# Identity, one weight load, the norm's small steps and the planner's limits in a planned attention and MLP kernel

## The chip, the cores and the metric

The kernel runs on one core of a Trainium2 chip. The metric is device time in microseconds (us). The kernel before takes 758.47 us, the median of 3 runs (757.53 to 758.52).

## The reference

`x` is 2048 rows of 512 numbers in bf16 (batch 1). Two branches work on it and a gate mixes them:

```
def _A_ref(x, wqkv, wo):          # 32 heads of 16
    q, k, v = split(x @ wqkv)
    p = softmax(q k^T * 16**-0.5)
    return concat(p v) @ wo
def _B_ref(x, w1, w2, w3, w4):    # F = 1792
    h  = gelu(layernorm(x) @ w1)
    x1 = x + shifted(h) @ w2      # four column quarters shifted by 1, -1, 2, -2 rows
    return x1 + gelu(layernorm(x1) @ w3) @ w4
g = sigmoid((x * gate_w).sum(-1)) # one number per row
out = g * _A_ref(x) + (1 - g) * _B_ref(x)
```

Gelu is the tanh approximation; the layer norms have no weights.

## The kernel before

**Tiling.** Everything is bf16 with f32 sums. The 2048 rows form 16 tiles of 128 (`x_sb`) and 4 chunks of 512. `xT` is x transposed: chunk 0 is made on TensorE by 16 transposes against a 128x128 identity (L1505), chunks 1 to 3 by DMA transposes (L150). A head unit is one chunk of queries by four heads; there are 4 x 8 = 32 units, each with 64 blocks of scores (16 key tiles by 4 heads, 128x512 each).

**The main loop.** TensorE (PE) computes two or three score blocks into a PSUM tile `stage` (L865); ScalarE (ACT) exponentiates the tile in one instruction into a ring of bf16 tiles (L1264); PE multiplies by the values and sums in `acc` (L1277). Not all blocks go to ACT. Whole groups of four heads go another way: their scores land in `dsc`, VectorE (DVE) turns them into 16-bit integers (L1082), three further terms come from adding a constant, on DVE (L1147) or on GpSimd (POOL, an INT64_ADD, L1145), and all four integer tiles (`quad`, `lent`, `more`, `xT` are the buffers) are read as bf16 by the value products, with plain (`vp`) or weighted values (`vw`).

**The rest of the work** is put between these slots: the projections, and the MLP branch. Its norms need per row mean and variance (`bn_stats`, `bn_aggr` at L440), the reciprocal root by an integer guess and three rounds of three steps (L460 to L466), the normalized tiles `xn` (L472) and their transposes `xnT`, four DMA transposes per chunk on SP's queue (L485). `ps_y` is a product of `xnT` with the first MLP weights (`w12`) or with `w3`.

**What sets the order.** A planner inside the kernel, run while the program is built, keeps a clock per engine (`free`), estimated costs and due times (`at`), and always takes the next step that could begin first; ties go by rank. It only writes the order down: on the chip each engine runs its instructions in that order, and waits on semaphores. DVE's small steps stand in one list `asides`, taken one at a time when their key says they are ready. `dma(t, own, count)` is its model of SP's queue, where each DMA has a fixed cost of issue. `rule(name)` reads limits per unit: from `RULES` for units 1 to 31, from `USUAL` for unit 0 and for names that `RULES` leaves out. `NEED` is how many blocks of a unit must be left for a group of it to go to DVE, `DLIM` how much work DVE may have queued, `CHAINS` how many groups may be open, `HURRY` and `AHEAD` when their steps gain rank, `MANY`, `PTS` and `SHORT` when value products come ahead of other work, `KEEP`, `BACK`, `PMAX` how add steps are shared between DVE and POOL. Where PE would idle too long, `fill` puts in matmuls with a zero tile.

**The start** is written out by hand. DMAs for the first tiles go out on SP and ACT (L123 to L125). DVE builds the identity from a ramp: it doubles a row of numbers seven times (L135), takes a 32x32 transposed column (L137) and compares in four strips (L140). POOL sets constant tiles meanwhile (L141 to L155), requests a set of programs (`load_library`, L163), which the INT64_ADD needs, and goes on. On SP the load of `wkv`'s value half (L148) waits for POOL's memset of wkv's last column (L146), and the input transposes (L150) for its memset of one element of xT (L147). PE runs 8 matmuls on a zero tile first (L1501), then the transposes against the identity.

**Weights.** `w12` is loaded at the start of the MLP (L562, L563), right ahead of the first four `xnT` transposes. `w3` (1792 KB) follows when its room is free (L764), `w4` (1792 KB) at L590.

Of the kernel before, what the change touches and what calls it, by code (L numbers as in the profile page):

```python
# [9 lines left out]

# [9 lines left out]
EPS = 1e-5  # L20
# [12 lines left out]
def kernel(  # L33
# [96 lines left out]
    ramp = const.tile([P, P], F32, name="ramp")  # L130
    row = const.tile([P, 32], F32, name="row")
    nc.vector.memset(ramp[:, 0:1], 0.0)
    w = 1
    while w < P:
        nc.vector.tensor_scalar(out=ramp[:, w:2 * w], in0=ramp[:, 0:w], scalar1=float(w), scalar2=None, op0=ALU.add)  # L135
        if w == 16:
            nc.vector.transpose(out=row[:], in_=ramp[:, 0:32])  # L137
        w *= 2
    for o in range(0, P, 32):
        nc.vector.tensor_scalar(out=ident[o:o + 32, :], in0=ramp[o:o + 32, :], scalar1=float(-o), scalar2=row[o:o + 32, 0:1], op0=ALU.add, op1=ALU.is_equal)  # L140
    nc.gpsimd.memset(zero[:], 0.0)  # L141
    nc.gpsimd.memset(vp0[:], 0.0)
# [20 lines left out]
    nc.gpsimd.load_library(library_config.all_libraries[1])  # L163
# [7 lines left out]
    for j in range(4):  # L171
# [10 lines left out]
        1: {'NEED': 12, 'AHEAD': 8, 'HURRY': 24, 'DLIM': 0.6, 'PTS': 6, 'CHAINS': 6, 'MAXD': 24, 'PMAX': 2, 'BACK': 0.6, 'KEEP': 0.6},  # L182
        2: {'NEED': 12, 'AHEAD': 8, 'HURRY': 24, 'DLIM': 0.6, 'PTS': 6, 'CHAINS': 6, 'MAXD': 24, 'PMAX': 2, 'BACK': 0.6, 'KEEP': 0.6},
        3: {'NEED': 12, 'AHEAD': 8, 'HURRY': 24, 'DLIM': 0.6, 'PTS': 6, 'CHAINS': 6, 'MAXD': 24, 'PMAX': 2, 'BACK': 0.6, 'KEEP': 0.6},
        4: {'NEED': 12, 'AHEAD': 8, 'HURRY': 24, 'DLIM': 0.6, 'PTS': 6, 'CHAINS': 6, 'MAXD': 24, 'PMAX': 2, 'BACK': 0.6, 'KEEP': 0.6},
        5: {'NEED': 12, 'AHEAD': 8, 'HURRY': 24, 'DLIM': 0.6, 'PTS': 6, 'CHAINS': 6, 'MAXD': 24, 'PMAX': 2, 'BACK': 0.6, 'KEEP': 0.6},
        6: {'NEED': 12, 'AHEAD': 8, 'HURRY': 24, 'DLIM': 0.6, 'PTS': 6, 'CHAINS': 6, 'MAXD': 24, 'PMAX': 2, 'BACK': 0.6, 'KEEP': 0.6},
        7: {'NEED': 12, 'AHEAD': 8, 'HURRY': 24, 'DLIM': 0.6, 'PTS': 6, 'CHAINS': 6, 'MAXD': 24, 'PMAX': 2, 'BACK': 0.6, 'KEEP': 0.6},
        8: {'NEED': 12, 'AHEAD': 8, 'HURRY': 24, 'DLIM': 0.6, 'PTS': 6, 'CHAINS': 6, 'MAXD': 24, 'PMAX': 2, 'BACK': 0.6, 'KEEP': 0.6},
        9: {'NEED': 12, 'AHEAD': 8, 'HURRY': 24, 'DLIM': 0.6, 'PTS': 6, 'CHAINS': 6, 'MAXD': 24, 'PMAX': 2, 'BACK': 0.6, 'KEEP': 0.6},  # L190
        10: {'NEED': 12, 'AHEAD': 8, 'HURRY': 24, 'DLIM': 0.6, 'PTS': 6, 'CHAINS': 6, 'MAXD': 24, 'PMAX': 2, 'BACK': 0.6, 'KEEP': 0.6},
        11: {'NEED': 12, 'AHEAD': 8, 'HURRY': 24, 'DLIM': 0.6, 'PTS': 6, 'CHAINS': 6, 'MAXD': 24, 'PMAX': 2, 'BACK': 0.6, 'KEEP': 0.6},
        12: {'NEED': 12, 'AHEAD': 8, 'HURRY': 24, 'DLIM': 0.6, 'PTS': 6, 'CHAINS': 6, 'MAXD': 24, 'PMAX': 2, 'BACK': 0.6, 'KEEP': 0.6},
        13: {'NEED': 12, 'AHEAD': 8, 'HURRY': 24, 'DLIM': 0.6, 'PTS': 6, 'CHAINS': 6, 'MAXD': 24, 'PMAX': 2, 'BACK': 0.6, 'KEEP': 0.6},
        14: {'NEED': 12, 'AHEAD': 8, 'HURRY': 24, 'DLIM': 0.6, 'PTS': 6, 'CHAINS': 6, 'MAXD': 24, 'PMAX': 2, 'BACK': 0.6, 'KEEP': 0.6},
        15: {'NEED': 12, 'AHEAD': 8, 'HURRY': 24, 'DLIM': 0.6, 'PTS': 6, 'CHAINS': 6, 'MAXD': 24, 'PMAX': 2, 'BACK': 0.6, 'KEEP': 0.6},
        16: {'NEED': 12, 'AHEAD': 8, 'HURRY': 24, 'DLIM': 0.6, 'PTS': 6, 'CHAINS': 6, 'MAXD': 24, 'PMAX': 2, 'BACK': 0.6, 'KEEP': 0.6},
        17: {'NEED': 12, 'AHEAD': 8, 'HURRY': 24, 'DLIM': 0.6, 'PTS': 6, 'CHAINS': 6, 'MAXD': 24, 'PMAX': 2, 'BACK': 0.6, 'KEEP': 0.6},
        18: {'NEED': 12, 'AHEAD': 8, 'HURRY': 24, 'DLIM': 0.6, 'PTS': 6, 'CHAINS': 6, 'MAXD': 24, 'PMAX': 2, 'BACK': 0.6, 'KEEP': 0.6},
        19: {'NEED': 12, 'AHEAD': 8, 'HURRY': 24, 'DLIM': 0.6, 'PTS': 6, 'CHAINS': 6, 'MAXD': 24, 'PMAX': 2, 'BACK': 0.6, 'KEEP': 0.6},  # L200
        20: {'NEED': 12, 'AHEAD': 8, 'HURRY': 24, 'DLIM': 0.6, 'PTS': 6, 'CHAINS': 6, 'MAXD': 24, 'PMAX': 2, 'BACK': 0.6, 'KEEP': 0.6},
        21: {'NEED': 12, 'AHEAD': 8, 'HURRY': 24, 'DLIM': 0.6, 'PTS': 6, 'CHAINS': 6, 'MAXD': 24, 'PMAX': 2, 'BACK': 0.6, 'KEEP': 0.6},
# [222 lines left out]
    ROOT = 0.18  # L425
    root_x, root_z = ([const.tile([P, NT if n == 0 else 4], F32, name=f"root_{k}{n}") for n in range(2)] for k in "xz")
    xns = {}

    def aside(cost, fn, key=None, shared=False):
        asides.append((cost, fn, key, shared))  # L430

    def ln_stats(n, t):
        st = {}

        def stats(end):
            st[0] = stat.tile([P, 6], F32, tag="bnst", name="st")
            nc.vector.bn_stats(out=st[0][:], in_=x_sb[t][:])
# [1261 lines left out]
```

## Time and profile before

| | |
|---|---|
| median of 3 runs | 758.47 us |
| profiled execution, its own time | 762.97 us |
| span of the profile | 761.2 us |
| mean granted TensorE clock | 0.986 |
| busy: PE, ACT, DVE, POOL | 736.3, 721.9, 674.0, 313.4 us |
| ACT's first score exponential begins | 13.72 us |
| PE waits for `xnT` | 4.5 us, 2 times |
| PE waits for the identity | 2.5 us, once |

In the profile a row of the waits gives engine, output and line, then what it waited for, the total in us, the times and the longest. A row in order of time gives start, duration, engine (SPq is the queue that issues SP's DMAs), line, operation, and in brackets the idle time before it. In the table by stretches the numbers behind each stretch are the busy us of PE, weight loads, DVE, ACT and POOL (with instruction counts), the granted clock of TensorE, the DMA share and GB/s. The ends of matmuls are modelled.

### The profile page before, as it was taken

Reading aid. Unit: us, or ns where it says so; the run is one execution under the profiler, and the core shown is the slowest. Engines: PE = TensorE matmul, PEld = TensorE weight load, DVE = VectorE, ACT = ScalarE, POOL = GpSimd, SP = SyncE. Lnnn points to the kernel's source line nnn. Section 1 sums busy time; section 2 is a strip of 40 time slices with the busy share of each in tenths; the row PEclk is TensorE's granted clock in tenths of the full one; section 3 lists DMA queues with packets and bytes.
Section 4 is the critical chain, followed back from the end, with each engine's and each line's share of the span. In section 5 each row is a group of like instructions: output and inputs, shape, how many; then the busy total and the mean of one; then the engine's idle time right before and its main releaser. Section 6 shows DMA issues by size and latency. Waiting matters only on the chain.

```text
span 761.2 us, 23457 instructions
## 1 busy us (share of the span) xinstructions
PE 736.3 (97%) x9805; PEld 225.3 (30%) x9806; DVE 674.0 (89%) x1231; ACT 721.9 (95%) x729; POOL 313.4 (41%) x329
## 2 busy tenths in 40 slices
PE   7999998999999998999999999999999999999997
PEld 3433322222332222232222232222322222232223
DVE  6989997999989996999999888899798989979974
ACT  4999998999999996899999999999999999999995
POOL 2024344445434323435544435453454544545540
PEclk9999998999999997999999999999999999999999
DMA  8300007101130025002001010000020000000001
GB/s 221 92 4 24 16 20 102 41 23 45 37 111 22 19 74 77 19 17 34 20 20 48 19 37 16 22 16 20 20 51 26 30 11 20 19 31 20 20 24 39
DMA packets 52306, 29.02 MB, mean 38 GB/s; under 512 B 36712, under 2 KB 47720, under 8 KB 52200
## 3 DMA queue, kind: packets, MB, share of 16 engines
q1 hardware_dynamic: 51240, 27.00, 14.8%
q8 instruction: 76, 1.25, 0.7%
q10 hardware_dynamic: 960, 0.52, 0.2%
q14 instruction: 30, 0.25, 0.1%
HBM read 17.17 MB, written 2.35 MB: 26 GB/s over the span
## 4 chain that ended last, share of the span: by engine, by line
PE 59%; DVE 18%; ACT 15%; issue 4%; SPq 2%; DMA 2%; DVEq 0%; ACTq 0%
PE acc L1277 20%; PE stage L865 18%; ACT ring L1264 11%; PE ps L323 8%; DVE quad L1082 4%; PE ps_y L323 4%; ACT pt L1264 3%; DVE more L1082 3%; PE stage L323 2%; SPq L485 2%; PE ps_o L323 2%; DVE xT L1082 1%; DMA xnT<-xn 1%; PE ps_q L323 1%; DVE oT L1386 1%
## 5 line engine op out<-in xcount | busy, mean ns | idle before, releaser
L1264 ACT ACTIVATE ring<-stage 128x1024 bf16<-128x1024 f32 (+1 forms) x648 | 641.1, 1116 | 18.0 <-PE dsc L865 11.8
L865 PE MATMUL stage<-qT,kT 16*128 16x512 bf16 (+2 forms) x1506 | 271.3, 384 | 5.7 <-ACT ring L1264 2.6
L865 PE MATMUL dsc<-qT,kT 16*128 16x512 bf16 (+1 forms) x566 | 219.3, 388 | 2.8 <-DVE quad L1082 1.7
L1082 DVE TENSOR_SCALAR quad<-dsc 128x512 int16<-128x512 f32 x242 | 161.3, 686 | 15.3 <-PE dsc L865 13.0
L865 PEld LDWEIGHTS <-kT 16*128 16x128 bf16 (+1 forms) x2072 | 73.5, 91 | 285.9 <-issue 260.7
L1277 PE MATMUL acc<-ring,vp 128*17 128x512 bf16 (+3 forms) x1408 | 125.6, 381 | 0.5 <-DVE accsb L1359 0.2
L1082 DVE TENSOR_SCALAR more<-dsc 128x512 int16<-128x512 f32 x147 | 98.0, 685 | 15.8 <-PE dsc L865 14.0
L1082 DVE TENSOR_SCALAR xT<-dsc 128x512 int16<-128x512 f32 x133 | 88.3, 684 | 8.4 <-PE dsc L865 7.7
L1145 POOL INT64_ADD quad<-quad x58 | 62.1, 1072 | 51.1 <-PE acc L1277 14.8
L1277 PEld LDWEIGHTS <-vp 128*17 128x17 bf16 (+1 forms) x2668 | 55.4, 89 | 78.4 <-issue 57.0
L323 PE MATMUL ps<-w,g2T 128*32 128x512 bf16 x896 | 67.4, 384 | 0.3 <-DVE ot L645 0.3
L323 PE MATMUL ps_y<-xnT,w 128*32 128x512 bf16 x704 | 56.3, 402 | 5.1 <-DMA xnT<-xn 4.5
L1145 POOL INT64_ADD xT<-quad x33 | 34.6, 1051 | 52.3 <-DVE more L1147 17.4
L1145 POOL INT64_ADD quad<-more x31 | 32.1, 1038 | 57.0 <-DVE quad L1147 25.4
L1277 PE MATMUL acc<-quad,vp 128*17 128x512 bf16 x516 | 48.4, 382 | 0.3 <-DVE quad L1147 0.3
L1277 PE MATMUL acc<-quad,vw 128*17 128x512 bf16 x492 | 47.2, 385 | 0.0
L1145 POOL INT64_ADD quad<-xT x28 | 29.0, 1038 | 38.2 <-DVE more L1147 16.4
L1145 POOL INT64_ADD more<-more x35 | 36.3, 1038 | 17.3 <-PE dsc L865 6.5
L1145 POOL INT64_ADD more<-quad x23 | 23.9, 1038 | 45.2 <-DVE quad L1147 27.2
L1277 PEld LDWEIGHTS <-vw 128*17 128x17 bf16 x1192 | 27.0, 89 | 38.2 <-issue 31.5
L323 PEld LDWEIGHTS <-w 128*32 128x32 bf16 x1152 | 25.3, 96 | 43.3 <-issue 26.0
L1264 ACT ACTIVATE pt<-stage 128x1024 bf16<-128x1024 f32 x34 | 31.4, 1094 | 1.2 <-PE stage L865 1.1
(148 smaller groups left out, 900.6 us busy)
## 6 DMA issues: line engine op xcount, KB each, us to landing
bcs<-rec_d SPq DMA_DIRECT2D x31, 256.0 KB
w<-in_B_w_dram SPq DMA_DIRECT2D x2, 1792.0 KB
x_sb<-in_A_x_dram SPq DMA_DIRECT2D x14, 128.0 KB
oT<-oT SPq DMA_DIRECT2D x112, 16.0 KB
out_dram<-ot SPq DMA_DIRECT2D x12, 128.0 KB
w<-in_B_w_dram SPq DMA_DIRECT2D x2, 512.0 KB
wkv<-in_A_wqkv_dram SPq DMA_DIRECT2D x1, 512.0 KB
wo_all<-in_A_wo_dram SPq DMA_DIRECT2D x8, 64.0 KB
```

The lines of the kernel that those rows point to most:

```text
L323: nc.tensor.matmul(out[j:j + 32, :], lhsT=lhsT[:, j:j + 32], rhs=rhs, tile_position=(0, j), **kwargs)
L485: nc.sync.dma_start(out=xnT[:, :, j * P:(j + 1) * P], in_=xns.pop((n, 4 * c + j))[:], transpose=True)
L865: nc.tensor.matmul(out, lhsT=kT[G][32 * j:32 * j + K, cc, o:o + P], rhs=qTs[(c, G)][32 * j:32 * j + K, a, lo:hi], start=True, stop=True, t ...
L1082: nc.vector.tensor_scalar(out=bits[:, r:r + wide, :], in0=dsc.rearrange("p (a c) -> p a c", c=CH), scalar1=SHIFT, scalar2=LOWEST, op0=ALU. ...
L1145: behind(nc.gpsimd.int64_add(out=words(to), in0=words(base["tile"]), in1=int(shift) * 0x0001000100010001))
L1264: nc.scalar.activation(out=pt[:, 0:w], in_=stages.pop(k)[:, 0:w], func=ACT.Exp, scale=LN2 / 128.0)
L1277: nc.tensor.matmul(accs[n][32 * j:32 * j + M, lo:hi], lhsT=lhsT, rhs=p, start=(kt == 0), stop=(kt == NT - 1), skip_group_check=True, tile_ ...
L1386: nc.vector.tensor_tensor(out=oT, in0=tiles["accsb"][:], in1=tiles["bcs"][:], op=ALU.mult)
```

## The change

Five edits. The identity is made on POOL by the library's helper (a memset and an AFFINE_SELECT, a masked copy by row and column), with the request for the set of programs ahead of it; DVE's ramp goes. The load of `w4` is written behind the transposes of the second norm's first chunk. Each `bn_aggr` and each root step gets a key `apart`, which lets the planner start it only 0.02 us after its estimate of the end of the step before. In the planner's model of SP's queue the transposes that follow the `w12` load cost 2.0 us each and not 1.3, until `at["heavy"]`. And the limits of units 1 to 31 are new (the 31 rows are alike, before and now).

```diff
-    ramp = const.tile([P, P], F32, name="ramp")
-    row = const.tile([P, 32], F32, name="row")
-    nc.vector.memset(ramp[:, 0:1], 0.0)
-    w = 1
-    while w < P:
-        nc.vector.tensor_scalar(out=ramp[:, w:2 * w], in0=ramp[:, 0:w], scalar1=float(w), scalar2=None, op0=ALU.add)
-        if w == 16:
-            nc.vector.transpose(out=row[:], in_=ramp[:, 0:32])
-        w *= 2
-    for o in range(0, P, 32):
-        nc.vector.tensor_scalar(out=ident[o:o + 32, :], in0=ramp[o:o + 32, :], scalar1=float(-o), scalar2=row[o:o + 32, 0:1], op0=ALU.add, op1=ALU.is_equal)
+    nc.gpsimd.load_library(library_config.all_libraries[1])
     nc.gpsimd.memset(zero[:], 0.0)
+    make_identity(nc, ident[:])
     nc.gpsimd.memset(vp0[:], 0.0)
...
-    nc.gpsimd.load_library(library_config.all_libraries[1])
...
-        1: {'NEED': 12, 'AHEAD': 8, 'HURRY': 24, 'DLIM': 0.6, 'PTS': 6, 'CHAINS': 6, 'MAXD': 24, 'PMAX': 2, 'BACK': 0.6, 'KEEP': 0.6},
+        1: {'NEED': 20, 'HURRY': 16, 'DLIM': 0.9, 'MANY': 10, 'PTS': 6, 'CHAINS': 3, 'MAXD': 24, 'PMAX': 2, 'BACK': 0.6, 'SHORT': -1, 'KEEP': 0.9},
...
+    def apart():
+        return state["aside"] + 0.02
+
...
-        aside(0.18, lambda end: nc.vector.bn_aggr(out=mvs[n][:, t, :], in_=st[0][:]))
+        aside(0.18, lambda end: nc.vector.bn_aggr(out=mvs[n][:, t, :], in_=st[0][:]), apart)
...
             for fn in (square, share_of, last if k == 2 else better):
-                aside(ROOT, fn)
+                aside(ROOT, fn, apart)
...
-        at["xnT", n, c, KT - 1] = at["xnfree"] = dma(state["t"], 1.3, 4) + XPOSE - 5.2 + MARGIN
+        at["xnT", n, c, KT - 1] = at["xnfree"] = dma(state["t"], 1.3 if state["t"] > at["heavy"] else 2.0, 4) + XPOSE - 5.2 + MARGIN
...
-        at["w12"] = state["t"] + 9.0
+        at["w12"] = at["heavy"] = state["t"] + 9.0
...
-        w4 = hw.tile([P, FT, D], BF16, tag="hw", name="w4")
-        nc.sync.dma_start(out=w4[:], in_=wview(B_w4))
-        at["w4"] = state["t"] + 16.0
         if w3 is None:
             yield lambda: 0.0 if retired["n"] == 3 else None
             w3 = load_w3()
         res = []
         yield from norm_T(1, 0, res)
+        w4 = hw.tile([P, FT, D], BF16, tag="hw", name="w4")
+        nc.sync.dma_start(out=w4[:], in_=wview(B_w4))
+        at["w4"] = state["t"] + 16.0
```

The order of the instructions at the places of which the prediction speaks (lines are those of each kernel's own file). POOL at the start, before: the end of the constant tiles, the copy of the identity, the request (the second row of kind ISA here is already the first INT64_ADD):

```order
L152 MEMSET pick 128x4
L154 MEMSET pick 1x1 x4
L155 CAST identf<-ident 128x128
L163 ISA
L421 MEMSET mhalf 128x1
L1535 COPY wkv<-gw 128x4
L1145 ISA lent<-quad_286 128x1024
```

and POOL at the start now:

```order
L131 ISA
L132 MEMSET zero 128x128
masks.py:197 MEMSET ident 128x128
masks.py:199 AFFINE_SELECT ident<-ident 128x128
L134 MEMSET vp_142 128x1024
L135 MEMSET vp_142 128x32
```

The request stood behind everything on POOL and is now first; the identity is POOL's third step, and the value tiles' memsets follow it.

SP's queue at the second norm, before: denominators (`den`), their reciprocals out and back (`rec_d`, `bcs`), w4 (`w_5794`), the transposes, four pieces of a head's output (`oT`):

```order
L1367 DMA den<-accsb 128x1x16
L1375 DMA rec_d<-rec 128x16
L1376 DMA bcs<-rec_d 128x1x512
L590 DMA w_5794<-in_B_w_dram 128x14x512
L485 DMA_TRANSPOSE xnT<-xn 128x4x128 x4
L1395 DMA oT_282<-oT 16x512 x4
```

and now:

```order
L1361 DMA den<-accsb 128x1x16
L1369 DMA rec_d<-rec 128x16
L1370 DMA bcs<-rec_d 128x1x512
L479 DMA_TRANSPOSE xnT<-xn 128x4x128 x4
L589 DMA w_5790<-in_B_w_dram 128x14x512
L1389 DMA oT_271<-oT 16x512 x4
```

The 1792 KB load has changed places with the four transposes; its neighbours are the same.

More of the change, by code (lines that the diff above doesn't have):

```diff
@@ L9 @@
 from concourse._compat import with_exitstack
+from concourse.masks import make_identity
 ACT = mybir.ActivationFunctionType
@@ L186 @@
[L186 to L197, printed above, removed]
@@ L213 @@
+        30: {'NEED': 20, 'HURRY': 16, 'DLIM': 0.9, 'MANY': 10, 'PTS': 6, 'CHAINS': 3, 'MAXD': 24, 'PMAX': 2, 'BACK': 0.6, 'SHORT': -1, 'KEEP': 0.9},
+        31: {'NEED': 20, 'HURRY': 16, 'DLIM': 0.9, 'MANY': 10, 'PTS': 6, 'CHAINS': 3, 'MAXD': 24, 'PMAX': 2, 'BACK': 0.6, 'SHORT': -1, 'KEEP': 0.9},
     }
```

52 lines of the change are left out of this document (31 added, 21 removed).

## The prediction

> **What bounds the kernel now.** I read the busy shares first, then the table of 10-us stretches, then the waits of each engine, and last the instructions in order of time around the long waits and at the start. The busy shares:
>
> ```profile
> span 761.2 us, 23457 instructions
> PE 736.3 (97%) x9805; PEld 225.3 (30%) x9806; DVE 674.0 (89%) x1231; ACT 721.9 (95%) x729; POOL 313.4 (41%) x329
> ```
>
> PE and ACT are both nearly full, and of the two ACT is the one whose share can be trusted, since the ends of matmuls are modelled. ACT's work is fixed in size (exponentials of the scores that DVE and POOL do not take), so time is lost where ACT stands idle, 761.2 - 721.9 = 39.3 us in all. Stretches with the busy time of PE, PEld, DVE, ACT, POOL, then the granted clock, DMA share and GB/s show where:
>
> ```profile
> 123.00:129.60 6.60, 4.68 (x59) 1.43 (x51) 5.65 (x10) 5.77 (x7) 4.25 (x4) 0.97 1.41 110
> 129.60:136.80 7.20, 7.16 (x60) 1.44 (x60) 3.91 (x6) 4.44 (x4) 2.37 (x3) 0.55 0.02 5
> 150.00:255.00 105.00, 102.19 (x1335) 31.20 (x1327) 99.41 (x177) 104.82 (x108) 48.92 (x47) 1.00 0.17 46
> 282.00:291.40 9.40, 9.18 (x104) 2.50 (x103) 9.40 (x21) 9.20 (x10) 3.74 (x4) 1.00 1.44 230
> 291.40:296.00 4.60, 1.90 (x15) 0.37 (x15) 1.86 (x5) 1.23 (x2) 2.46 (x3) 0.68 0.21 45
> 296.00:301.00 5.00, 5.00 (x41) 1.01 (x37) 3.30 (x6) 3.45 (x4) 0.00 (x0) 0.50 0.01 1
> 301.00:306.00 5.00, 5.00 (x45) 1.14 (x41) 2.60 (x7) 2.65 (x3) 1.49 (x2) 0.50 0.04 6
> 306.00:312.00 6.00, 5.96 (x77) 1.48 (x70) 5.57 (x14) 5.65 (x6) 2.44 (x3) 0.94 0.12 44
> 343.70:437.50 93.80, 93.24 (x1249) 26.09 (x1249) 86.20 (x142) 93.30 (x96) 45.14 (x43) 1.00 0.11 28
> ```
>
> In 150 to 255 ACT is idle 0.18 us of 105, in 343.7 to 437.5 0.50 of 93.8: there it is the bound. Between 123.0 and 136.8 it is idle 13.80 - 5.77 - 4.44 = **3.59 us**, and between 282 and 312 30.00 - 9.20 - 1.23 - 3.45 - 2.65 - 5.65 = **7.82 us**. In both PE stops first and then runs at a granted clock of 0.50 to 0.68, so that ACT starves although PE reads as full. PE's waits and its instructions name the cause:
>
> ```profile
> PE ps_y L323 <- DMA xnT<-xn: 4.5, 2, 2.7
> PE ps_t L1505 <- DVE ident L140: 2.5, 1, 2.5
> 129.65 0.62 PE L323 MATMUL ps_y<-xnT,w 128*32 128x512 bf16 x4 [1.77 <-DMA xnT<-xn]
> 294.10 0.62 PE L323 MATMUL ps_y<-xnT,w 128*32 128x512 bf16 x4 [2.71 <-DMA xnT<-xn]
> ```
>
> Both times the first matmuls on a chunk's transposed norm wait for the DMA transposes, 1.77 and 2.71 us. SP's queue shows why they are late:
>
> ```profile
> 116.81 0.39 SPq L562 DMA_DIRECT2D w<-in_B_w_dram  x1
> 117.79 7.96 SPq L485 DMA_TRANSPOSE xnT<-xn  x4
> 178.00 5.15 SPq L485 DMA_TRANSPOSE xnT<-xn  x4
> 186.18 0.39 PE L323 MATMUL ps_y<-xnT,w 128*32 128x512 bf16 x4
> 279.40 0.42 SPq L590 DMA_DIRECT2D w<-in_B_w_dram  x1
> 279.87 10.29 SPq L485 DMA_TRANSPOSE xnT<-xn  x4
> ```
>
> With nothing ahead, four transposes issue in 5.15 us and are read by PE 8.18 us after the first began (186.18 - 178.00), without a wait. Behind the first-layer weights they take 7.96 us to issue, behind w4 10.29 us, and PE reads them 11.86 and 14.23 us after the first.
>
> **The change, part by part.** *w4 behind the transposes.* In SP's order the w4 load now stands behind the four transposes of the second norm's first chunk, which have only small transfers just ahead of them. Their landing goes from 14.23 us back to at most 8.18. The order keeps ten score slots on PE between issue and first use, before and now; a slot costs ACT 93.8 / 96 = 0.98 us in the stretch from 343.7, so they cover 9.8 us. The wait and its slow clock should go: **-7.8 us**. What is late instead is w4, by about 5 us; it is first read by the second layer's last product, after the Gelu that starts at 333.18, some 50 us later:
>
> ```profile
> 333.18 1.28 ACT L1241 ACT_TABLE_LOAD   x1
> ```
>
> With that cover gone it would cost those 5 us.
>
> *Transposes costed at 2.0 us behind the first weights.* The queue keeps the loads ahead of the transposes. The planner now expects them later: PE's order has 14 score slots between their issue and first use where it had 10, and they are the program's own work brought forward. Four slots are 3.9 us, the wait was 1.77, so it is covered with about 2 us over: **-3.6 us**. If the landing slips by as much again, nothing is gained here; a loss would need a landing 3.9 us later.
>
> [...]
>
> *Identity on GpSimd.* The start, in order of time:
>
> ```profile
> 0.73 0.20 POOL L141 MEMSET zero<- 128x128 bf16 x1 [0.29 <-POOLq L1683]
> 1.19 4.31 DVE L135 TENSOR_SCALAR ramp<-ramp 128x1 f32<-128x1 f32 x5
> 1.19 3.60 PE L1501 MATMUL warm<-ring 128*128 128x512 bf16 x8 [1.19 <-DVE ramp L132]
> 2.16 1.28 ACT L1507 ACT_TABLE_LOAD   x1 [2.16 <-issue]
> 3.77 0.40 POOL L146 MEMSET wkv<- 128x1 bf16 x1
> 4.21 0.37 SPq L148 DMA_DIRECT2D wkv<-in_A_wqkv_dram  x1
> 7.28 1.87 PE L1505 MATMUL ps_t<-ident,x_sb 128*128 128x128 bf16 x16 [2.50 <-DVE ident L140]
> 7.37 0.29 POOL L155 CAST identf<-ident 128x128 f32<-128x128 bf16 x1 [1.77 <-DVE ident L140]
> 7.76 0.10 POOL L421 MEMSET mhalf<- 128x1 f32 x1
> 14.40 0.40 PE L323 MATMUL ps_v<-wkv,xT 128*32 128x256 bf16 x8 [0.71 <-DVE qT L1543]
> 20.18 0.51 SPq L169 DMA_DIRECT2D gw<-in_gate_w_dram  x1
> 25.39 0.20 POOL L1535 COPY wkv<-gw 128x4 bf16<-128x4 bf16 x1 [17.52 <-DMA wo_pad<-in_A_wo_dram]
> 49.41 1.04 POOL L1145 INT64_ADD lent<-quad  x1 [23.82 <-DVE quad L1147]
> ```
>
> Removed are thirteen short DVE instructions from the ramp to the four comparisons, which end at 7.2; PE stood idle 2.50 us for them after its warm-up (1.19 + 3.60 = 4.79). Added on POOL are a memset (0.20 us, as zero) and a selection over the same 128x128 (0.29 us, as identf), now behind the request for the set of programs. How long that request holds the selection the trace does not show: a plain memset ran right behind it at 7.76, and the first instruction that needs the set came only at 49.41, so it took under 41.7 us. From below, PE cannot start before 4.79, so the gain is at most **2.5 us**; that is the case if it costs what ACT's table load costs (1.28). From above, 41.7 us would make the start some 36 us later. The nearest row I see is a fetch into the crowded start: gw's, 25.39 - 20.18 = 5.21 us from issue to use. By it the identity stands at 0.73 + 5.21 + 0.20 + 0.29 = 6.4 and PE starts 0.8 us earlier: **-0.8 us**. [...]
>
> Behind the selection on POOL's queue stand the memsets of the value tiles, of wkv's last column and of xT, and behind these, on SP's queue, the load of wkv's value half (4.21 before), the three input transposes and all later loads. They slip by about 5.5 us (6.4 - 0.9). The cover is the time until their first reader: wkv was issued at 4.21 and read at 14.40, 10.2 us later, so 3.9 us would remain (13.6 - 9.7) where a fetch like gw's needs 5.21. Up to 1.3 us could show; but wkv's half now comes first on a queue that has been idle since the first tiles, so I take **0**, with 0 to +5.5 (no cover at all) as bounds.
>
> *Steps set apart, new limits.* Counting instructions of both orders: 149 groups of four heads that DVE and POOL exponentiate become 148, so ACT gets two more 1024-wide exponentials; at the pitch of the first 34 (31.51 / 34 = 0.93) that is **+1.9 us**.
>
> ```profile
> 13.72 31.51 ACT L1264 ACTIVATE pt<-stage 128x1024 bf16<-128x1024 f32 x34 [1.07 <-PE stage L865]
> L1145 POOL INT64_ADD quad<-quad x58 | 62.1, 1072 | 51.1 <-PE acc L1277 14.8
> 45.00:752.40 707.40, 691.14 (x9218) 205.74 (x9211) 634.58 (x1113) 687.81 (x691) 307.95 (x296) 0.99 0.14 32
> ```
>
> DVE does 148 of the add steps instead of 153, POOL 296 instead of 294 (1.07 us each), neither of them the bound. Setting a bn_aggr or root step behind the end of the one before lets other DVE work between them: nothing on the path. Between 45 and 752.4 ACT is idle 707.40 - 687.81 = 19.6 us, 11.4 of it in the two places. The 8.2 us left are scattered waits, and the new order may halve them or add half again: **0**, bounds -4 to +4. PE's order has 216 filler matmuls where it had 184, which hide in waits.
>
> Sum: -7.8 - 3.6 - 0.8 + 1.9 = **-10.3 us**. The profiled execution took 762.97 us (span 761.2), so it would take 752.7. It is 4.5 us above the median of the runs, 758.47. If the runs have the same stalls, they come to 758.47 - 10.3 = 748.2; if all of the 4.5 sits in the two stalls, to 752.7. I lay a third of it there: **749.7 us**.
>
> **Rivals.** *One stall stays.* The loads still stand ahead of the first transposes, and the slots that cover them are a plan. Then 758.47 - 10.3 + 3.6 = 751.8 with the first, or 756.0 with the second left. For it: both stalls came from plans that thought they covered them. Against it: 2.1 and 1.6 us to spare.
>
> *New stalls from the new limits.* Every due time shifts; a PE gap of 1.8 us cost 3.6 us, one of 2.7 us 7.8. Two new gaps take 7 us back: about 756.5. Against it: in the two long stretches of the table, 199 us together, no PE wait took the clock below 1.00.
>
> *The request holds POOL too long.* Mechanism: the selection waits, PE has no identity, the memsets behind it hold SP's loads. Each us past 6.0 (where PE starts as before) is a us of ACT idle. Slower than before begins where the request takes about 5.2 + 10.3 = 15.5 us; at 20 us the time is 764. For it: nothing in the trace bounds it below 41.7. Against it: every fetch at the start lands within 6 us.
>
> *The change does not do what it says:* w4 could be held by hT's readers anyway and the transposes pass unhindered before too. The 10.29 us issue against 5.15 excludes that.
>
> **How the numbers follow.** Forecast (both stalls gone, start about as before) 0.65; one stall stays 0.14; new stalls 0.12; the request too long, slower 0.07; no effect 0.02. The range from 743 to 757 holds the forecast's bounds (749.7 - 1.7 for the start, - 4 for the limits, - 1; and the same limits upward) and most of the two rivals that take part of the gain back. A measurement of this kernel tells a change of 0.2%, 1.5 us, from none. Slower than 760.0 is the third rival and little else: 0.07. Within 0.2%: the far ends of rivals one and two, and no effect, 0.06. Faster: 0.87.
>
> **What would show it.** Right: PE's wait for xnT gone from its list or under 0.3 us; granted clock 1.00 in the stretches of both norms; the four transposes of the second norm issued in about 5.2 us; ACT idle about 27 us in all. PE's first transposes between 4.8 and 7.3, and the value half of wkv issued near 9.7. Wrong: a clock near 0.5 after any later gap, a PE start past 9 us, or waits for wkv or xT on PE between 14 and 30.

## The result, and the profile after

The changed kernel takes **750.98 us**, the median of four runs (748.32 to 751.88), against 758.26 us (757.53 to 758.52, four runs) for the kernel before: a ratio of **0.990, 95% interval 0.9874 to 0.9926**. The forecast was 749.7. Its profiled execution took 748.32 us, the shortest of its four, where the one of before (762.97) was longer than all its others; so the two profiles stand 14.65 us apart, and the medians 7.3.

First the busy shares after, then the table by stretches (start and end, length, busy us of PE, weight loads, DVE, ACT and POOL with instruction counts, granted clock, DMA share, GB/s) around the two norms:

```profile
span 746.5 us, 23512 instructions
PE 727.2 (97%) x9826; PEld 226.5 (30%) x9826; DVE 659.7 (88%) x1209; ACT 723.0 (97%) x731; POOL 316.4 (42%) x333
...
112.00:125.00 13.00, 12.93 (x164) 3.86 (x166) 12.68 (x22) 13.00 (x15) 7.49 (x10) 1.00 0.96 144
125.00:137.00 12.00, 11.88 (x162) 3.28 (x159) 11.99 (x23) 12.00 (x14) 3.99 (x4) 1.00 0.10 29
280.00:292.00 12.00, 11.92 (x156) 3.44 (x153) 11.89 (x26) 11.35 (x13) 6.24 (x6) 1.00 0.31 98
292.00:312.00 20.00, 19.30 (x256) 5.86 (x252) 19.80 (x41) 19.90 (x21) 4.16 (x4) 1.00 0.06 19
```

The clock is 1.00 in all four rows, where before it fell to 0.50 and 0.55. At the first norm ACT is never idle (25.00 of 25 us; before, 3.59 us idle between 123.0 and 136.8). At the second it is idle 32.00 - 11.35 - 19.90 = 0.75 us (before, 7.82 between 282 and 312). Over the whole span its idle time went from 39.3 to 746.5 - 723.0 = 23.5 us.

SP's queue at both norms, and the matmuls on the transposed norm, in order of time:

```profile
112.75 0.51 SPq L557 DMA_DIRECT2D w<-in_B_w_dram  x1
113.30 10.20 SPq L479 DMA_TRANSPOSE xnT<-xn  x4
...
129.05 0.61 PE L314 MATMUL ps_y<-xnT,w 128*32 128x512 bf16 x8
...
270.68 5.17 SPq L479 DMA_TRANSPOSE xnT<-xn  x4
275.97 0.51 SPq L589 DMA_DIRECT2D w<-in_B_w_dram  x1
...
281.80 0.83 PE L314 MATMUL ps_y<-xnT,w 128*32 128x512 bf16 x12
```

Neither row of PE has a wait behind it. At the second norm the transposes issue in 5.17 us, as where nothing is ahead of them. At the first norm they still stand behind two loads and issue more slowly than before (10.20 us against 7.96), but are read only 15.75 us after the first began (129.05 - 113.30), where the old order wanted them within 10.1 (11.86 less the wait of 1.77).

The start after, POOL, PE and ACT in order of time:

```profile
0.90 0.20 POOL L132 MEMSET zero<- 128x128 bf16 x1 [0.45 <-POOLq L1677]
...
1.19 3.60 PE L1495 MATMUL warm<-ring 128*128 128x512 bf16 x8 [1.19 <-DVE ring L130]
1.32 0.29 POOL masks.py:199 TENSOR_SCALAR_AFFINE_SELECT ident<-ident 128x128 bf16<-128x128 bf16 x1
...
4.58 1.40 PE L1499 MATMUL ps_t<-ident,x_sb 128*128 128x128 bf16 x16
5.81 0.59 PE L1505 MATMUL warm<-ring 128*128 128x512 bf16 x2
...
6.54 0.60 PE L1512 MATMUL ps_q<-xT,wq 128*128 128x256 bf16 x4
8.68 31.51 ACT L1258 ACTIVATE pt<-stage 128x1024 bf16<-128x1024 f32 x34 [0.50 <-PE stage L859]
```

and the rows of before that answer to the two warm-up matmuls behind the transposes and to the query matmuls:

```profile
8.94 1.06 PE L1511 MATMUL warm<-ring 128*128 128x512 bf16 x2
...
10.22 1.06 PE L1518 MATMUL ps_q<-xT,wq 128*128 128x256 bf16 x4
```

The request holds next to nothing: the memset of `zero` begins at 0.90 where it began at 0.73, the selection runs 0.42 us later, the identity stands at 1.61, and PE goes from its warm-up into the transposes without a stop. The load of `wkv` slips from 4.21 to 4.89 only. ACT's first score exponential moves from 13.72 to 8.68, **5.04 us**. That is more than PE's start gained: 7.28 - 4.58 = 2.70 us. The other 2.3 us come from the speed of the matmuls behind it: before, four query matmuls took 1.06 us, now 0.60.

PE does not begin at full speed in either kernel. The eight warm-up matmuls take 3.60 us in both, 0.45 each, where two of the same form take 0.59 at 5.81 in the changed kernel and 1.06 at 8.94 before. In the changed kernel PE is at full speed once the transposes are done; before, with its gap of 2.50 us, it works at about half speed until some 13 us. The clock column reads 1.00 there, but the trace holds no record of the clock ahead of 13.17 us in the kernel before and of 4.80 in the changed one, and without a record the column reads 1.00.

The parts add up: start -5.04, first norm -3.59, second norm -7.07, ACT's own work 723.0 - 721.9 = +1.1: together **-14.6 us** of the 14.65 between the profiles. ACT's other waits hardly changed. This sum is of two single executions; the timed runs below give smaller terms.

### The profile page after: what moved, and what is told of

The parts are those of the page before. It is cut to its first block, busy times and chain, and to the rows that moved or that the text cites. A ratio compares the mean times of both kernels' runs of the same rounds, so it can differ in the third digit from the quotient of the medians.

```text
span 746.5 us, 23512 instructions
## 1 busy us (share of the span) xinstructions
PE 727.2 (97%) x9826; PEld 226.5 (30%) x9826; DVE 659.7 (88%) x1209; ACT 723.0 (97%) x731; POOL 316.4 (42%) x333
## 4 chain that ended last, share of the span: by engine, by line
PE 58%; DVE 19%; ACT 17%; issue 5%; POOL 0%; DVEq 0%; POOLq 0%; ACTq 0%
PE acc L1271 20%; PE stage L859 17%; ACT ring L1258 14%; PE ps L314 7%; DVE quad L1076 5%; PE ps_y L314 4%; ACT pt L1258 3%; PE stage L314 3%; DVE more L1076 2%; PE ps_o L314 2%; DVE xT L1076 2%; DVE quad L1141 1%; PE ps_q L314 1%; DVE st L431 1%; DVE oT L1380 1%
## 5 line engine op out<-in xcount | busy, mean ns | idle before, releaser
L859 PE MATMUL dsc<-qT,kT 32*128 32x512 bf16 (+1 forms) x566 | 217.4, 384 | 0.0
L859 PEld LDWEIGHTS <-kT 32*128 32x128 bf16 (+1 forms) x2072 | 74.5, 91 | 281.5 <-issue 259.7
L1271 PE MATMUL acc<-ring,vp 128*17 128x512 bf16 (+2 forms) x1412 | 125.5, 378 | 0.9 <-DVE accsb L1353 0.4
L1076 DVE TENSOR_SCALAR more<-dsc 128x512 int16<-128x512 f32 x134 | 89.3, 683 | 7.2 <-PE dsc L859 6.1
L1076 DVE TENSOR_SCALAR xT<-dsc 128x512 int16<-128x512 f32 x119 | 79.3, 685 | 9.9 <-PE dsc L859 9.1
L1139 POOL INT64_ADD more<-quad x35 | 36.6, 1047 | 69.6 <-DVE quad L1141 20.7
L1139 POOL INT64_ADD xT<-quad x27 | 28.4, 1056 | 43.5 <-DVE more L1141 17.3
L1076 DVE TENSOR_SCALAR lent<-dsc 128x512 int16<-128x512 f32 x68 | 44.9, 685 | 1.1 <-PE dsc L859 0.5
L1139 POOL INT64_ADD xT<-xT x31 | 32.2, 1040 | 30.3 <-DVE more L1141 8.6
L1139 POOL INT64_ADD quad<-xT x20 | 21.2, 1061 | 46.9 <-PE acc L1271 18.4
```

The source lines that it names most:

```text
L859: nc.tensor.matmul(out, lhsT=kT[G][32 * j:32 * j + K, cc, o:o + P], rhs=qTs[(c, G)][32 * j:32 * j + K, a, lo:hi], start=True, stop=True, t ...
L1076: nc.vector.tensor_scalar(out=bits[:, r:r + wide, :], in0=dsc.rearrange("p (a c) -> p a c", c=CH), scalar1=SHIFT, scalar2=LOWEST, op0=ALU. ...
L1139: behind(nc.gpsimd.int64_add(out=words(to), in0=words(base["tile"]), in1=int(shift) * 0x0001000100010001))
L1271: nc.tensor.matmul(accs[n][32 * j:32 * j + M, lo:hi], lhsT=lhsT, rhs=p, start=(kt == 0), stop=(kt == NT - 1), skip_group_check=True, tile_ ...
```

## The experiments

The difference after minus before joins three kinds of edit: the identity, `w4`'s place, and three edits that only the planner sees (the steps set apart, transposes costed at 2.0 us, the limits). The first two can be made on the kernel before without moving anything in PE's order: the traces show the same sequence of matmuls. Each kernel was timed beside the kernel before on the same chip; its median there was 758.06, 758.61 and 758.05 us in the three groups.

### The identity alone

```diff
# on the kernel before
-    ramp = const.tile([P, P], F32, name="ramp")
...
+    nc.gpsimd.load_library(library_config.all_libraries[1])
     nc.gpsimd.memset(zero[:], 0.0)
+    make_identity(nc, ident[:])
...
-    nc.gpsimd.load_library(library_config.all_libraries[1])
```

> The kernel before with the identity on GpSimd behind the early request, nothing else; the order on TensorE is the same as before. Theory (the start is worth more than its wait, because TensorE also works at half speed after the gap of 2.5 us): the first score exponential begins at 8.7 us instead of 13.7, the four query matmuls take 0.60 us and not 1.06, and the time falls by 5 us, to about 753. Rival (only the wait goes, 2.5 us, the half speed is an accident of the one profile): about 756.

Measured: **754.53 us** (754.19 to 756.64, six runs), ratio 0.9958 (0.9946 to 0.9970), so -3.5 us; its first exponential stands at 8.50 us in the profile. In the profile the move is 5.2 us, in the timed runs 3.5, between the two theories; why they differ is seen under the longer warm-up below. Both stalls are still there: PE waits 3.4 us in all for `xnT`.

The reverse, the changed kernel with DVE's ramp and the late request:

```diff
# on the changed kernel
-    nc.gpsimd.load_library(library_config.all_libraries[1])
+    ramp = const.tile([P, P], F32, name="ramp")
...
     nc.gpsimd.memset(zero[:], 0.0)
-    make_identity(nc, ident[:])
...
+    nc.gpsimd.load_library(library_config.all_libraries[1])
```

> The changed kernel with the identity back on VectorE and the request back where it was; the order on TensorE is that of the changed kernel. Theory: first exponential at 13.7 instead of 8.7, 5 us slower than the changed kernel, about 756. Rival: 2.5 us slower, about 753.5.

Measured: 753.62 us (751.82 to 756.29, six runs), ratio 0.9943 (0.9926 to 0.9961), against 0.9900 and 0.9887 of the changed kernel in its two timings: the identity is worth 0.43 to 0.56% of 758, **3.3 to 4.2 us**, the same from this side. Its profile, PE and ACT at the start in order of time, then two stretches of its table:

```profile
7.29 0.83 PE L1508 MATMUL ps_t<-ident,x_sb 128*128 128x128 bf16 x12 [2.51 <-DVE ident L140]
...
10.15 1.06 PE L1521 MATMUL ps_q<-xT,wq 128*128 128x256 bf16 x4
12.88 31.51 ACT L1267 ACTIVATE pt<-stage 128x1024 bf16<-128x1024 f32 x34 [0.50 <-PE stage L868]
...
5.00:10.00 5.00, 2.34 (x21) 1.66 (x21) 3.88 (x18) 0.60 (x1) 0.83 (x8) 0.81 0.98 229
10.00:15.00 5.00, 4.28 (x48) 2.41 (x45) 2.03 (x5) 2.88 (x5) 0.00 (x0) 0.85 1.12 234
```

The gap and the slow matmuls are back, and here the clock column shows them too, at 0.81 and 0.85: 2 x 0.19 x 5.00 + 2 x 0.15 x 5.00 = 3.4 us at half speed.

### Closing the gap without moving the identity

If the slow matmuls behind the gap come from it, a longer warm-up should remove them though the identity is as late as before.

```diff
# on the kernel before
-    WARM = 8
+    WARM = 14
```

> The kernel before with 14 warm-up matmuls in place of 8; the identity stays on VectorE and comes as late as before, at 7.2 us. Theory (the gap of 2.5 us before the first transposes makes TensorE work at half speed until 13 us): the gap shrinks to about 1 us, the query matmuls take 0.60 us, the first exponential begins 2.3 us earlier, at 11.4, and the time falls by 2.3 us. Rival (the speed at the start has another cause): first exponential at 13.7, same time.

Its profile, PE and ACT at the start:

```profile
1.19 5.97 PE L1501 MATMUL warm<-ring 128*128 128x512 bf16 x14 [1.19 <-DVE ramp L132]
...
9.40 0.60 PE L1518 MATMUL ps_q<-xT,wq 128*128 128x256 bf16 x4
...
11.54 31.51 ACT L1264 ACTIVATE pt<-stage 128x1024 bf16<-128x1024 f32 x34 [0.50 <-PE stage L865]
```

The transposes start at 7.25, as late as before, the query matmuls take 0.60, and the first exponential moves from 13.72 to 11.54: -2.2 us with the wait for the identity merely filled by matmuls. The fourteen warm-up matmuls themselves still run at half speed, 5.97 / 14 = 0.43 us each; PE, kept at work, is at full speed when the transposes come (0.83 us for the first twelve). So the gap puts off full speed, or takes it away again, and does not only cost its own 2.5 us.

How much it costs differs between executions. The kernel with `w4` alone (next section) has the start of the kernel before, gap included:

```profile
10.18 0.60 PE L1518 MATMUL ps_q<-xT,wq 128*128 128x256 bf16 x4
...
12.32 18.67 ACT L1264 ACTIVATE pt<-stage 128x1024 bf16<-128x1024 f32 x20 [0.50 <-PE stage L865]
```

Here full speed is back for the query matmuls. In the four profiles with the gap the first exponential begins at 12.32, 12.88, 12.94 and 13.72 us, in the nine with the identity on GpSimd at 8.37 to 9.18. The profile of before is the latest of its four; the means are 4.3 us apart, and that agrees with the 3.3 to 4.2 of the timed runs better than 5.04 does.

The timing of the longer warm-up does not carry its gain: 757.53 us (755.86 to 767.1, twelve runs), ratio 1.0008 (0.9983 to 1.0033). Against the four profiles with the gap, 11.54 is 0.8 to 2.2 us earlier, and the runs of this kernel scatter too widely for that to show; whether a gain is lost later was not settled.

### w4 alone

```diff
# on the kernel before
-        w4 = hw.tile([P, FT, D], BF16, tag="hw", name="w4")
-        nc.sync.dma_start(out=w4[:], in_=wview(B_w4))
-        at["w4"] = state["t"] + 16.0
...
         yield from norm_T(1, 0, res)
+        w4 = hw.tile([P, FT, D], BF16, tag="hw", name="w4")
+        nc.sync.dma_start(out=w4[:], in_=wview(B_w4))
+        at["w4"] = state["t"] + 16.0
```

> The kernel before with w4's load behind the four transposes of the second norm, nothing else; the order on TensorE is the same as before. Theory (stall and the slow clock after it are the price, 7.8 us in the profile): no wait for xnT near 291, clock 1.00 from 282 to 312, span 7.8 us shorter, and in the timed runs 5 to 8 us less, 750 to 753. Rival (the timed runs hardly have the slow clock; the profile of before was 4.5 us above their median): 2.5 to 4 us less, 754 to 756.

Measured: **752.20 us** (751.53 to 752.36, four runs), ratio 0.9918 (0.9906 to 0.9931), so -5.9 us. Its profile: what is left of PE's waits for `xnT` (total, times, longest), and the stretches of both norms.

```profile
PE ps_y L323 <- DMA xnT<-xn: 1.0, 1, 1.0
...
125.00:137.00 12.00, 11.00 (x153) 3.19 (x150) 10.80 (x20) 11.05 (x12) 4.43 (x5) 1.00 0.09 19
292.00:312.00 20.00, 17.99 (x239) 5.50 (x231) 19.77 (x40) 18.03 (x18) 7.94 (x8) 1.00 0.06 18
```

The second stall is gone. The first one, which nothing here touched, was 1.0 us in this execution and did not lower the clock.

The reverse, `w4` ahead of the transposes in the changed kernel (the same three lines moved back):

> The changed kernel with w4 ahead of the transposes again; TensorE's order is that of the changed kernel, with ten slots to cover the transposes as before. Theory (the order on the queue is what removed the second stall): the wait of 2 to 3 us for xnT is back, then a slow clock, and the time rises by 5 to 6 us, to about 757. Rival (the new order covers the late transposes anyway): 751.

Measured: 755.08 us (median of twelve, 753.95 to 762.59), ratio 0.9973 (0.9946 to 1.0000): +5.6 us over the changed kernel timed beside it. Three of the twelve stood near 762.5, at a mean clock of 0.982 where the others had 0.993 to 0.995; no profile shows where. The waits and the stretch:

```profile
PE ps_y L314 <- DMA xnT<-xn: 3.6, 1, 3.6
...
280.00:292.00 12.00, 8.40 (x78) 2.03 (x79) 6.27 (x12) 5.87 (x6) 3.09 (x3) 0.72 0.44 49
```

Wait and slow clock return together. New limits and steps set apart do not cover this stall; in both directions `w4`'s place decides it.

### Is it the gap or the slow clock behind it?

The prediction priced a stall at its gap and the slow clock after it. This kernel keeps the loads and the wait of before and gives PE 14 groups of filler matmuls to do just ahead of the second norm's first product. They multiply by a tile of zeros and add to an accumulator that is open, so nothing is left out of the computation.

```diff
# on the kernel before, in front of ps_y
+        if key == ("z", 0, 0):
+            acc = list(accs.values())[0]
+            for _ in range(14):
+                strips(acc[:], lhsT=zero[:], rhs=wq[:, 0, :], start=False, stop=False, skip_group_check=True)
```

> The kernel before with 14 filler matmuls (zero weights, four strips each, about 3.1 us at full speed) ahead of the first matmul on xnT in the second norm; w4 stays ahead of the transposes, so the data is as late as before. Theory (most of the second stall's price is the slow clock after TensorE's gap, not the gap): the granted clock stays at 1.00 from 282 to 312, ScalarE loses about 3 us there and not 7.8, and the time falls by 3 to 4.5 us, to about 754.5. Rival (the wait itself is the price): 758, unchanged.

Measured: **754.75 us** (754.09 to 755.38, six runs), ratio 0.9952 (0.9938 to 0.9966), so -3.3 us. In its profile, SP's queue and PE in order of time and the stretch, then the same stretch of the kernel before:

```profile
275.71 10.23 SPq L485 DMA_TRANSPOSE xnT<-xn  x4
...
287.07 3.19 PE L323 MATMUL acc<-wq,zero 128*32 128x512 bf16 x56
290.09 0.39 PE L323 MATMUL ps_y<-xnT,w 128*32 128x512 bf16 x4
...
282.00:312.00 30.00, 27.79 (x368) 9.03 (x364) 27.11 (x54) 25.05 (x26) 11.62 (x11) 1.00 0.36 49
```

```profile
282.00:312.00 30.00, 27.04 (x266) 6.49 (x266) 22.74 (x50) 22.18 (x22) 10.13 (x10) 0.77 0.52 89
```

The transposes were as slow to issue as before, 10.23 us against 10.29, and their reader started right behind the filler, 14.4 us after the first of them (290.09 - 275.71) against 14.23. PE worked on zeros through that time, and the clock stayed at 1.00 instead of 0.77. ACT is idle 30.00 - 25.05 = 4.95 us here and 30.00 - 22.18 = 7.82 before. Of the 5.9 us that `w4`'s place is worth in the timed runs, 3.3 came back; the intervals, 0.34 to 0.62% against 0.69 to 0.94% of 758, allow no finer statement than about half. So about half of the price of this stall was the slow clock after it, and it came with the gap of 2.7 us: 0.77 over the stretch with the gap, 1.00 with the gap filled.

### Both edits together, and the first stall

```diff
# on the kernel before
-    ramp = const.tile([P, P], F32, name="ramp")
...
+    make_identity(nc, ident[:])
...
-        w4 = hw.tile([P, FT, D], BF16, tag="hw", name="w4")
...
         yield from norm_T(1, 0, res)
+        w4 = hw.tile([P, FT, D], BF16, tag="hw", name="w4")
```

> The kernel before with two edits, GpSimd's identity and w4 behind the transposes; TensorE's order is the old one. Alone they gave 758.06 - 754.53 = 3.5 us and 758.06 - 752.20 = 5.9 us. Theory (they add, since they lie 270 us apart on a path where ScalarE is the bound): 748.6, some 2 us faster than the whole change; then the new limits, the set-apart steps and the dearer transposes cost time together. Rival (the whole change is these two, and they share a part): 751.

Measured: **749.69 us** (748.14 to 751.53, four runs), ratio 0.9878 (0.9860 to 0.9897), -8.9 us where the single edits add up to -9.4. The changed kernel, timed again beside it:

> The changed kernel as it is, on the same chip as the others of this call: 751.0 by its first four runs, with the profiled one below the others. If its start and both norms are free of slow clock again and the time still lies 2 us over the run with both edits, the loss is in the new order.

Measured: 749.48 us (748.79 to 751.57, four runs), ratio 0.9887 (0.9869 to 0.9905). The three planner edits together are worth nothing that can be measured: 0.2 us.

And yet they remove the first stall, which the two edits leave. Its profile in the kernel with both edits:

```profile
PE ps_y L314 <- DMA xnT<-xn: 1.7, 1, 1.7
...
125.00:137.00 12.00, 12.00 (x131) 2.83 (x127) 8.72 (x15) 9.00 (x9) 2.31 (x4) 0.74 0.03 6
```

What that stall costs can be measured with PE's order as it was, by loading the first-layer weights as soon as their memory is free, some 70 us ahead of the norm, at 42.45 us (where their pool opens, and no longer in the function of the MLP):

```diff
# on the kernel with both edits
-        w12 = pools["g"].tile([P, FT, CH], BF16, tag="g", name="w12")[:, 0:2 * KT, :].rearrange("p (kt h) c -> p kt (h c)", kt=KT)
-        nc.sync.dma_start(out=w12[:, :, 0:D], in_=wview(B_w1))
-        nc.sync.dma_start(out=w12[:, :, D:2 * D], in_=wview(B_w2))
+        w12 = pools["w12"]
...
+            w12 = pools["w12"] = pools["g"].tile([P, FT, CH], BF16, tag="g", name="w12")[:, 0:2 * KT, :].rearrange("p (kt h) c -> p kt (h c)", kt=KT)
+            nc.sync.dma_start(out=w12[:, :, 0:D], in_=wview(B_w1))
+            nc.sync.dma_start(out=w12[:, :, D:2 * D], in_=wview(B_w2))
```

> As the run with both edits, and the first MLP weights are loaded when their pool opens (near 45 us), so that nothing large stands ahead of the first transposes; TensorE's order is still the old one. Theory (the first stall's wait of 1.0 to 1.8 us, now and then with a slow clock, goes): 1 to 2.5 us less than the run with both edits, about 747, without a wait for xnT near 129. Rival (the first stall costs nothing in the timed runs): equal to the run with both edits.

Measured: **747.49 us** (746.97 to 747.76, four runs), ratio **0.9855 (0.9841 to 0.9870)**, 2.2 us below the kernel with both edits and 2.0 below the changed kernel, with the smallest scatter of all. Its slowest run is faster than the fastest of either, though the intervals of the ratios overlap. Its transposes, their reader and the stretch:

```profile
112.14 5.51 SPq L476 DMA_TRANSPOSE xnT<-xn  x4
123.16 0.39 PE L314 MATMUL ps_y<-xnT,w 128*32 128x512 bf16 x4
...
125.00:137.00 12.00, 12.00 (x168) 3.29 (x160) 11.66 (x22) 12.00 (x14) 4.52 (x5) 1.00 0.05 12
```

With nothing ahead of them the four transposes issue in 5.51 us and PE does not wait. So the first stall is worth about 2 us, and the planner edits, which remove it too, give about as much back elsewhere. It is the more variable of the two: in the six profiles that have it its wait is 0.8 to 1.8 us, and only the two of 1.7 us and more show a slow clock. Two places for what is given back are visible, though the runs do not price them: ACT works longer (723.0 against 721.2 us here), and in one of its two profiles the changed kernel has a new slow clock late in the program, that of its second timing:

```profile
695.00:700.00 5.00, 4.61 (x47) 1.16 (x39) 4.95 (x8) 4.86 (x6) 3.13 (x4) 0.87 0.03 5
700.00:705.00 5.00, 5.00 (x60) 1.29 (x57) 2.60 (x6) 3.51 (x5) 2.08 (x2) 0.78 0.07 18
...
700.13 1.90 PE L314 MATMUL ps<-w,g2T 128*32 128x512 bf16 x16
```

and in that of its first, where the same instructions run at full speed:

```profile
695.00:700.00 5.00, 4.61 (x55) 1.39 (x54) 5.00 (x9) 4.86 (x6) 3.31 (x4) 1.00 0.02 2
699.13 1.05 PE L314 MATMUL ps<-w,g2T 128*32 128x512 bf16 x16
```

PE is busy 4.61 us of 695 to 700 in both, and the two gaps that its rows name there are 0.16 and 0.23 us; once the clock fell behind them and once it did not. The spans differ by 748.4 - 746.5 = 1.9 us.

### The planner's edits one by one

Each was put alone on the kernel with both edits, and the limits were taken back from the changed kernel. All three re-plan the whole order from the first norm on, so a difference is that of two plans and not the isolated price of an edit. The limits on their own, and the other pairs, were not run.

```diff
# on the kernel with both edits
-        aside(0.18, lambda end: nc.vector.bn_aggr(out=mvs[n][:, t, :], in_=st[0][:]))
+        aside(0.18, lambda end: nc.vector.bn_aggr(out=mvs[n][:, t, :], in_=st[0][:]), apart)
...
-                aside(ROOT, fn)
+                aside(ROOT, fn, apart)
```

> The kernel before with GpSimd's identity, w4 behind, and the steps set apart, nothing else. The new key shifts the whole plan: ScalarE gets 791,573 columns and not 781,333. Theory (ScalarE's work is the bound): 10,240 columns at 31.51 us for 34 x 1024 are 9.3 us more than the run with the two edits, about 758; the first norm has 10 slots as there. Rival (setting the steps apart pays for it on VectorE): 750 or less.

Measured: 759.35 us (753.48 to 762.66, twelve runs), ratio 1.0013 (0.9989 to 1.0037), +9.7 over the kernel with both edits and near the theory's 758.

```diff
# on the kernel with both edits
-        at["xnT", n, c, KT - 1] = at["xnfree"] = dma(state["t"], 1.3, 4) + XPOSE - 5.2 + MARGIN
+        at["xnT", n, c, KT - 1] = at["xnfree"] = dma(state["t"], 1.3 if state["t"] > at["heavy"] else 2.0, 4) + XPOSE - 5.2 + MARGIN
...
-        at["w12"] = state["t"] + 9.0
+        at["w12"] = at["heavy"] = state["t"] + 9.0
```

> The kernel before with GpSimd's identity, w4 behind, and the dearer transposes behind the first weights, nothing else. 18 slots stand before the first use in the first norm, 8 in the second, and ScalarE gets 787,477 columns. Theory: no wait for xnT near 129 (2 us less), 6,144 columns more (5.6 us), a wait of about 0.4 us in the second norm: about 753. Rival (the wait is all that counts): 747.

Measured: 757.78 us (757.42 to 763.94, twelve runs), ratio 1.0002 (0.9985 to 1.0020), +8.1; neither the theory's 753 nor the rival's 747. The busy shares, and the place where PE newly stops or slows, first with the steps set apart:

```profile
PE 733.6 (97%) x9818; PEld 228.7 (30%) x9818; DVE 655.9 (87%) x1195; ACT 729.4 (96%) x731; POOL 301.4 (40%) x319
...
285.00:290.00 5.00, 4.13 (x46) 0.95 (x42) 5.00 (x9) 4.83 (x6) 0.18 (x1) 0.85 0.10 39
290.00:295.00 5.00, 5.00 (x40) 0.87 (x40) 4.28 (x8) 3.92 (x5) 1.90 (x2) 0.50 0.03 7
```

and with the costed transposes (its profile, 763.94 us, is the longest of its twelve runs):

```profile
PE 739.4 (97%) x9826; PEld 226.6 (30%) x9826; DVE 662.9 (87%) x1207; ACT 727.8 (95%) x728; POOL 306.9 (40%) x322
...
PE dsc L856 <- DVE xT L1073: 3.5, 2, 3.0
280.00:285.00 5.00, 5.00 (x46) 1.10 (x45) 3.98 (x10) 3.49 (x3) 2.08 (x2) 0.59 0.28 87
```

Both plans leave ACT more work (729.4 and 727.8 us; 721.8 in the kernel with both edits), since DVE and POOL do fewer exponentials, and each has a new place with a slow clock: behind a wait of 3.0 us for DVE with the costed transposes, and with the steps set apart behind a stretch in which PE was idle 0.87 us in all (5.00 - 4.13, in two gaps of 0.34 and 0.52). The wait for the first norm's transposes is gone in both, and that weighs little against the rest. The limits:

```diff
# on the changed kernel, units 1 to 31
-        1: {'NEED': 20, 'HURRY': 16, 'DLIM': 0.9, 'MANY': 10, 'PTS': 6, 'CHAINS': 3, 'MAXD': 24, 'PMAX': 2, 'BACK': 0.6, 'SHORT': -1, 'KEEP': 0.9},
+        1: {'NEED': 12, 'AHEAD': 8, 'HURRY': 24, 'DLIM': 0.6, 'PTS': 6, 'CHAINS': 6, 'MAXD': 24, 'PMAX': 2, 'BACK': 0.6, 'KEEP': 0.6},
```

> The changed kernel with the old limits of units 1 to 31. The columns that ScalarE exponentiates are as many as in the changed kernel (783,381 per partition), with 13 slots for the first and 9 for the second norm's transposes. Theory (ScalarE's work sets the time, the limits only matter through it and through stalls): equal to the changed kernel within 2 us, 748 to 752. Rival (the new limits carry part of the gain): 754 or more.

Measured: **762.76 us** (759.92 to 763.81, six runs), ratio 1.0053 (1.0033 to 1.0072): slower than before, and some 12 us over the changed kernel by the ratios (1.0053 less 0.9900 and 0.9887 is 1.53 and 1.66% of 758). My theory of 748 to 752 fell. The profile tells where it goes: ACT's last exponentials and a stretch behind them.

```profile
714.83 24.26 ACT L1258 ACTIVATE ring<-stage 128x1024 bf16<-128x1024 f32 x21 [0.37 <-PE dsc L859]
...
755.00:760.00 5.00, 2.80 (x20) 0.72 (x12) 2.50 (x4) 0.00 (x0) 0.00 (x0) 0.50 0.30 105
```

and in the changed kernel:

```profile
731.73 7.31 ACT L1258 ACTIVATE ring<-stage 128x1024 bf16<-128x1024 f32 x6 [0.44 <-PE stage L859]
```

ACT ends its exponentials at 714.83 + 24.26 = 739.09 with the old limits and at 731.73 + 7.31 = 739.04 with the new. From there to the end of the span it is 22.3 us with the old and 7.5 with the new. With the old limits pieces of the output projection are left for the end, where PE and DVE take turns on them (at 749.37, 0.75 us of DVE behind a wait of 1.15 for PE, 1.90 us a piece), and then the clock is at 0.50. The limits' part, in this plan, is to bring that work in under the exponentials.

## Why the prediction was right, and where not

**The second stall, -7.8.** Right in mechanism and place: the transposes issue in 5.17 us, PE does not wait, the clock stays at 1.00. Worth 7.07 us between the profiles, and 5.9 and 5.6 in the two timed pairs. The term was read from an execution 4.5 us longer than the median, and came out 1.9 too large.

**The first stall, -3.6.** Gone, by the larger distance from issue to reader as the prediction said. The margin of "about 2 us over" was needed: the four transposes took 2.2 us longer to issue than before. It measures 3.59 between the profiles, but 2.2 timed, by the early load of the weights. The prediction laid a third of the profile's extra 4.5 us on the stalls; with 1.9 too much on the second and 1.4 on the first it was nearer to three quarters.

**The price of a stall.** To take it from the rows, gap and slow clock together, was right: filling the gap of 2.7 us with products of zero brought back 3.3 us with the transposes as late as before. The gaps of the two stalls alone are 1.77 + 2.71 = 4.5 us; timed, the stalls were 5.9 + 2.2 = 8.1. In the profile of before the clock was at half from 129.22 to 136.05 us and from 293.06 to 306.71, that is for 6.83 and 13.65 us, two and four times 3.41; in the other profiles the tables by stretches give slow stretches of about 3.4, 6.8, 13.7 and 20.5 us. A slow stretch can be longer than the wait that goes with it: at the first norm 6.83 us with a wait of 1.77 (before) and 6.7 with one of 1.70 (both edits).

**The identity, -0.8.** This is the step that failed: the term was mis-sized on both sides. The nearest row chosen, 5.21 us from the issue of gw's load to its use, was the wrong one, and its bracket names `wo_pad`'s load, not gw's, as what ended the wait; the request moved POOL's start by 0.17 us, and the selection ran at once. The selection itself took 0.29 us; whether it belongs to the set that is loaded, no run here shows. And "at most 2.5 us", worked out from PE's wait, left out what follows the wait: PE's half speed behind the gap. I had read the slow clock behind both later stalls and not allowed for it behind the third wait of about the same length, because the clock column there read 1.00. The rows could have told: each of the eight warm-up matmuls over 512 columns took 0.45 us (3.60 / 8), and the score matmuls over as many columns take 0.39 for two. The term was -5.04 between the profiles and -3.5 timed, where the profile of before has the latest start of the four with the gap.

**The slip of SP's loads.** Reckoned at 5.5 us with a cover of 3.9; it was 0.7, since it followed from the same wrong hold on POOL. Taken as 0, and 0 it was.

**Limits and steps set apart, 0.** The terms of what the planner sees, -3.6 + 0 + 1.9, add up to -1.7; timed, the three edits together gave -0.2. That is near, but the picture was wrong. They were taken as a gentle shift of scattered waits, -4 to +4. The partial plans that were run are 8 to 13 us slower; only the three together come out even, and that is luck as far as the prediction goes. ACT's extra work was +1.1 us, not +1.9. The rival of new stalls came true in part: one of two profiles has a slow clock near 700.

**The sum.** Between the profiles -14.6 where -10.3 was forecast, nearly all from the start. The medians moved by 7.3 (and 9.1 in the second timing), where 8.8 was forecast. So 749.7 came out close partly by luck, through errors that offset each other: the start was worth 2.7 us more than said in the timed runs (3.5 - 0.8), the two stalls 1.8 less (3.3, of which 1.5 had been allowed for), and the new plan gives back about the 1.9 us that stood in the sum for ACT's work, though not by that work alone.

## What to carry to other kernels

Price a PE stall by the rows before and after it, not by its wait: where the same matmul on the same shape takes 1.06 us instead of 0.60, the slow stretch here cost about as much as the gap, and filler work through the gap, even on zeros, saved that part while the data was as late as ever. Take such a price from several profiles: the same gap at the start cost 1.4 us more in one execution than in another. Put a large load behind the small transfers that something waits for (5.9 us here), or so far ahead that it has long landed (2.2). Changing the inputs of a planner is changing the whole order, so an edit of the program's own and a re-tuned plan should be timed apart; here two edits that left PE's order alone held all of the gain that could be measured, and a third of that kind gave 2 us more.

## What was not expected of the hardware

- The clock column can read 1.00 over a stretch in which matmuls run at half speed: at the start of the kernel before, 1.06 us for a group that takes 0.60, and over the warm-up matmuls, 0.45 us each where two of the same form take 0.59 in the changed kernel. Ahead of the trace's first record of the clock, at 13.17 us in the profile of before and 4.80 in that of the changed kernel, the column says nothing. In the profile with DVE's ramp put back the stretch from 10 to 15 reads 0.85.
- Waits of 0.8 to 1.2 us at the first norm left the clock at 1.00, and behind waits of 1.7 us and more at the norms it fell to 0.50 (125 to 130 with both edits, 285 to 290 with `w4` ahead again, 296 to 306 before). But behind two gaps of 0.16 and 0.23 us, near 697, it fell in one profile (0.87 from 695 to 700, 0.78 from 700 to 705) and not in another (1.00), with the same instructions; in the plan with the steps set apart it fell to 0.50 behind 0.87 us of scattered idle time. So in these profiles the length of a single gap did not decide. The changes of the clock that the trace of before records, from 13.17 us on, lie 34, 2, 46, 4 and 133 times 3.41 us apart; whether the place of a gap between such steps matters, no run here tests.
- The first GpSimd selection behind the request for the set of programs ran 0.42 us after the first memset behind it began. What the request costs, and when, these runs do not show.
- Four transposes of the same size took 5.2 to 5.5 us to issue alone, and 8.0 to 10.4 us right behind large loads on the same queue.
